# Window attention with its gradients on one core: the order of the first loads and of the weight products

## The chip, the core and the metric

The kernel runs on one core of a Trainium2 chip. The core has five engines that run their own streams of instructions in order: TensorE (PE, matrix products and transposes by product), VectorE (DVE), ScalarE (ACT), GpSimd (POOL) and SyncE (SP). SP, ACT and POOL can issue transfers between the chip's main memory and the core's memory (SBUF), and SP and ACT also transfers that transpose. PE writes to PSUM, which this kernel uses as a ring of eight banks; DVE and ACT copy from there to SBUF. The metric is the time of one execution in microseconds on the device: the median of the runs.

## The reference, cut to what matters

The input x has 256 x 256 positions of 384 channels in bf16, and attention runs in windows of 8 x 8 positions. Wanted are the output, and the gradients of x, wqkv and wo for a given gradient of the output.

```
xw  = x cut into windows of 64 positions           # 1024 windows
q, k, v = split(xw @ wqkv)                          # each 64 x 384
p   = softmax(q @ k.T * 384 ** -0.5)
out = (p @ v) @ wo, put back in place
out, grads of (x, wqkv, wo) by jax.vjp for grad_out
```

## The kernel before, in words

**Products of weights.** The kernel never forms q, k and v. With A = scale * Wq Wk^T the scores are x A x^T, and with B = Wv Wo the output is p (x B); the gradient uses the transposes AT and BT in the same way. So the weights are loaded once (`w_sb` holds wqkv with column blocks 0, 1, 2 for q, k, v; `wo_sb` holds wo), turned block by block (`turn_blocks`, nine PE transposes, three copies), and multiplied (`weight_product`, nine products of 384 columns, three copies): BT_sb from wo_sb and the turned v block, A_sb from the turned q and k blocks. B_sb and AT_sb are BT_sb and A_sb turned once more (`weight_rest`, L113, called by the first `step` at L368).

**Quads.** Eight windows, 512 positions in four pieces of 128, make a quad; there are 128 quads (L410), numbered from 0 here as in the code. For each quad the x piece `xq` and the gradient piece `dq` are loaded, four transfers each, and both are needed turned as well (`xT`, `dT`, channels on partitions). `load_turn` (L142) lets SP issue a transposing transfer for that, unless the quad's number is below G_ON_PE (for dT) or X_ON_PE (for xT), L408. With 2 and 1, PE turns the gradients of quads 0 and 1 and the x of quad 0, in `turn_on_pe` (L150): twelve transposes, copies by DVE and ACT in turn (L87).

**The work on a quad.** `project` with kind 0 makes z from BT_sb and dT, with kind 1 makes y from A_sb and xT: nine products of 512 columns each, copied by ACT into `yz`. `gather` (DVE) packs them into `zy`, and `to_tokens` (L182, SP, a transposing transfer) turns them into `tok`. `scores` multiplies yz and xT, `soft` is the softmax and its gradient on DVE, `uv` multiplies xT with B_sb and AT_sb, and `attend` makes the outputs, which POOL stores. Sums for the weight gradients run in between (`gf_rows`, `gf_halves`) from the fourth step on, and the end makes the weight gradients of them.

**The loop.** `step` (L485 to L490) does the second half of quad i-1 (`attend`), the middle of quad i (scores, softmax, uv) and the projections of quad i+1, and loads quad i+4 ahead (AHEAD = 4), though not in the first step. Before each step SP issues the transposing transfers of quad i+2 and then `to_tokens` of quad i.

**The start.** All engines are under a manual schedule (L454): each runs its instructions in the order in which the program names them. ACT issues v, wo and q (L76 to L78). SP issues quad 0's gradient, the k columns, quad 0's x (L128 to L131), then x of quads 1 and 2 (L140), the turn of quad 1's x (L147), x of quads 3 and 4 (L140), and in the loop the turns of quad 2 and tok of quad 0 (L184). POOL clears the sums, then makes a copy of one column (L132) that holds it until quad 0's first x piece is there, and then issues the gradients of quads 1 to 4 (L138). PE makes seven products of zeros (`warm_up`), then turns v, turns quad 0's gradient, makes BT_sb, turns q, makes z of quad 0, turns k, turns quad 0's x, makes A_sb, turns quad 1's gradient, makes y of quad 0, and enters the loop, where it turns BT_sb and A_sb first.

Of the kernel before, what the change touches and what calls it, by code (L numbers as in the profile page):

```python
# [11 lines left out]
BF16 = mybir.dt.bfloat16  # L12
# [11 lines left out]
def kernel(  # L24
# [47 lines left out]
    def columns(k):  # L72
        return slice(k * C, (k + 1) * C)

    def fetch_weights():
        nc.scalar.dma_start(out=w_sb[:, :, columns(2)], in_=w_in[:, :, columns(2)])  # L76
        nc.scalar.dma_start(out=wo_sb[:], in_=wo.rearrange("(m p) n -> p m n", p=P))
        nc.scalar.dma_start(out=w_sb[:, :, columns(0)], in_=w_in[:, :, columns(0)])  # L78

    def warm_up(n):  # L80
        zero = B_sb[:].rearrange("p m c -> p (m c)")[:, 0:4 * P]
# [11 lines left out]
    def turn_blocks(dst, src, first=0, act=True):  # L93
        for k in range(CK):
            pt = ring.tile([P, C], BF16, tag="r", name="pt")
            for m in range(CK):
                nc.tensor.transpose(pt[:, m * P:(m + 1) * P], src[:, m, (first + k) * P:(first + k + 1) * P], ident[:])  # L97
            copy_out(k if act else 0, dst[:, k, :], pt[:])

    def weight_product(dst, left, right, sc):  # L100
        for mr in range(CK):
            pc = ring.tile([P, C], F32, tag="r", name="pc")
            for mc in range(CK):
                nc.tensor.matmul(pc[:], lhsT=left[:, mc, mr * P:(mr + 1) * P], rhs=right[:, mc, :],  # L104
                                 start=(mc == 0), stop=(mc == CK - 1))
            if sc is not None and mr % 2:
                nc.scalar.activation(out=dst[:, mr, :], in_=pc[:], func=ACT.Copy, scale=sc)
            elif sc is not None:
                nc.vector.tensor_scalar(out=dst[:, mr, :], in0=pc[:], scalar1=sc, scalar2=None, op0=ALU.mult)
            else:  # L110
                copy_out(mr, dst[:, mr, :], pc[:])

    def weight_rest():  # L113
        turn_blocks(B_sb, BT_sb)
        turn_blocks(AT_sb, A_sb)

    def windows(ap, st, first, count=2):
        row, col = st["at"]
        return ap[0, row + WIN * first:row + WIN * (first + count), col:col + WIN, :]
# [4 lines left out]
    def load_first(st):  # L124
        st["xq"] = xq = grp.tile([P, QUAD, C], BF16, tag="xq", name="xq", bufs=2 * GQ + 5)
        st["dq"] = dq = qp.tile([P, QUAD, C], BF16, tag="dq", name="dq", bufs=6)
        for t in range(QUAD):
            nc.sync.dma_start(out=dq[:, t, :], in_=windows(grad_out, st, 2 * t))  # L128
        nc.sync.dma_start(out=w_sb[:, :, columns(1)], in_=w_in[:, :, columns(1)])
        for t in range(QUAD):  # L130
            nc.sync.dma_start(out=xq[:, t, :], in_=windows(x, st, 2 * t))  # L131
        nc.gpsimd.tensor_copy(out=spare[:], in_=xq[:, 0, 0:1])  # L132

    def load(st):
        st["xq"] = xq = grp.tile([P, QUAD, C], BF16, tag="xq", name="xq", bufs=2 * GQ + 5)
        st["dq"] = dq = qp.tile([P, QUAD, C], BF16, tag="dq", name="dq", bufs=6)
        for t in range(QUAD):
            nc.gpsimd.dma_start(out=dq[:, t, :], in_=windows(grad_out, st, 2 * t))  # L138
        for t in range(QUAD):
            (nc.gpsimd if st["i"] == AHEAD + 1 else nc.sync).dma_start(out=xq[:, t, :], in_=windows(x, st, 2 * t))  # L140
# [9 lines left out]
    def turn_on_pe(st, src, dst):  # L150
        for t in range(QUAD):
            pt = ring.tile([P, CK, P], BF16, tag="r", name="pt")
            for m in range(CK):
                nc.tensor.transpose(pt[:, m, :], st[src][:, t, m * P:(m + 1) * P], ident[:])
            copy_out(t, st[dst][:, t, :, :], pt[:])
# [6 lines left out]
    def project(st, kind, mo):  # L162
        if kind == 0 and mo == 0:
            st["yz"] = qp.tile([P, CK, QUAD, 4, WT], BF16, tag="yz", name="yz", bufs=1)
        yz = st["yz"]
        wgt, src = ((BT_sb, st["dT"]), (A_sb, st["xT"]))[kind]
        pj = ring.tile([P, QUAD, 2, WT], F32, tag="r")
        for m in range(CK):
            product(pj[:].rearrange("p t w k -> p (t w k)"), wgt[:, m, mo * P:(mo + 1) * P], src[:, :, m, :],
                    m == 0, m == CK - 1)  # L170
        if kind == 0:
            ENG[EV["z"][mo]](out=yz[:, mo, :, 0:4:3, :], in_=pj[:])  # L172
        else:
            ENG[EV["y"][mo]](out=yz[:, mo, :, 1:3, :], in_=pj[:])  # L174

    def gather(st, kind):
        if kind == 0:
            st["zy"] = qp.tile([P, 2, CK, QUAD, 2, WT], BF16, tag="zy", name="zy")
        src = st["yz"][:, :, :, 0:4:3, :] if kind == 0 else st["yz"][:, :, :, 1:3, :]
        nc.vector.tensor_copy(out=st["zy"][:, kind, :, :, :, :], in_=src)  # L180
# [180 lines left out]
    def step(c, b, a, ahead):  # L361


        def on(st):
            return (lambda f, *r: f(st, *r)) if st is not None else (lambda f, *r: None)
        C_, B, A = on(c), on(b), on(a)
        if b is not None and c is None:
            weight_rest()  # L368
        B(scores)
        B(soft, 0)  # L370
        B(uv, 0, 0)
        B(uv, 0, 1)
        B(soft, 1)
        B(uv, 1, 0)
        B(uv, 1, 1)
        B(soft, 2)
        B(soft, 3)
        B(uv, 2, 0)
        B(uv, 2, 1)
        B(uv, 3, 0)  # L380
        B(uv, 3, 1)
        B(soft, 4)
        for mo in range(CK):
            A(project, 0, mo)
        B(soft, 5)
        if b is not None and not b["on_pe"]:
            turn(b)
        if b is not None and b["i"] == 1:
            turn_blocks(woT_sb, wo_sb, act=False)
        if ahead is not None:  # L390
            load(ahead)
        A(gather, 0)
        for mo in range(CK):
            A(project, 1, mo)
        for rows in range(1 if a is not None else 2):
            if fill:
                gf_rows(*fill.pop(0))
        if b is not None and b["on_pe"]:
            turn(b)
        slots = attention(c) if c is not None else iter(())  # L400
        for t in range(QUAD):
            if t == 2:
                A(gather, 1)
            next(slots, None)
        for rest in slots:
            pass

    G_ON_PE, X_ON_PE = 2, 1  # L408
    EV = {"z": "AAA", "y": "AAA", "u": "AAAA", "v": "AAAA", "o": "AAAA", "U": "DDDD", "W": "AAAA", "d": "DADAA"}
    quads = [(row, col) for col in range(0, W, WIN) for row in range(0, H, 2 * WIN * QUAD)]  # L410
    n = len(quads)
# [41 lines left out]

    with tc.manual_schedule(engines=MANUAL):  # L454
        spare = sm.tile([P, 1], BF16, name="spare", bufs=1)
        fetch_weights()
        warm_up(7)
        nc.scalar.copy(out=spare[:], in_=B_sb[:, 0, 0:1])
        make_identity(nc, ident[:])
        nc.gpsimd.memset(GF_acc[:], 0.0)  # L460
        load_first(sts[0])
        load(sts[1])
        load(sts[2])
        load_turn(sts[0])
        load_turn(sts[1])
        load(sts[3])
        load(sts[4])
        turn_blocks(wT[2], w_sb, 2 * CK)
        turn_on_pe(sts[0], "dq", "dT")
        weight_product(BT_sb, wo_sb, wT[2], None)  # L470
        turn_blocks(wT[0], w_sb, 0)
        for mo in range(CK):
            project(sts[0], 0, mo)
        turn_blocks(wT[1], w_sb, CK)
        turn_on_pe(sts[0], "xq", "xT")
        gather(sts[0], 0)
        weight_product(A_sb, wT[0], wT[1], scale)
        turn_on_pe(sts[1], "dq", "dT")
        for mo in range(CK):
            project(sts[0], 1, mo)  # L480
        gather(sts[0], 1)
        held = []
        last = None
        get = lambda i: sts[i] if 0 <= i < n else None
        for i in range(n + 1):  # L485
            if 0 <= i < n - 2:
                load_turn(sts[i + 2])
            if 0 <= i < n:
                to_tokens(sts[i])
            step(get(i - 1), get(i), get(i + 1), get(i + AHEAD) if i else None)  # L490
            if i > 0:
                held.append(sts[i - 1])
                sts[i - 1] = None
            if held and i == n:
                last = gf_final(held)
            elif len(held) == GQ:
                fill.extend((held, f, ma) for f in range(2) for ma in range(CK))
                held = []
        while fill:
            gf_rows(*fill.pop(0))  # L500
        weight_gradients(last)
# [30 lines left out]
```

## Time and profile before

| what | value |
|---|---|
| runs, median (lowest to highest of 3) | 1904.01 us (1903.54 to 1905.97) |
| the profiled execution | 1900.77 us |
| its span, first to last instruction | 1899.0 us |
| PE busy | 1889.7 us, 100% of the span, 22413 products |
| DVE busy | 1664.4 us, 88% |
| ACT busy | 1526.1 us, 80% |
| POOL busy | 862.7 us, 45% |
| DMA, mean rate | 215 GB/s, 407.69 MB |
| transposing transfers, median to landing | dT 7.9 us, xT 7.5 us, tok 7.7 us |
| plain loads, median to landing | x 4.1 us (SP), gradient 5.9 us (POOL) |
| first transfers: issued, landed | v 0.74, 4.0; wo 1.19, 5.2; q 1.73, 8.1; k 3.39, 9.0 |
| quad 0's gradient, four pieces | issued from 0.74, landed 4.3 to 7.9 |
| quad 0's x, four pieces | issued from 4.02, landed 9.3 to 10.1 |
| scores of quad 0 on PE | start at 19.86 us |
| projections of quad 1 | z at 24.49 us, y at 26.44 us |

How to read it: all times behind the third line are counted from the span's start. A transfer has a moment of issue on its engine and a moment of landing, at which the waiting engine is told. PE's busy time is that of products whose ends are modelled, so that a busy PE need not be at its peak; the chain of waits tells better what sets the end.

### The profile page before, as it was taken

Reading aid. Unit: us, or ns where it says so; the run is one execution under the profiler, and the core shown is the slowest. Engines: PE = TensorE matmul, PEld = TensorE weight load, DVE = VectorE, ACT = ScalarE, POOL = GpSimd, SP = SyncE. Lnnn points to the kernel's source line nnn. Section 1 sums busy time; section 2 is a strip of 40 time slices with the busy share of each in tenths; the row PEclk is TensorE's granted clock in tenths of the full one; section 3 lists DMA queues with packets and bytes.
Section 4 is the critical chain, followed back from the end, with each engine's and each line's share of the span. In section 5 each row is a group of like instructions: output and inputs, shape, how many; then the busy total and the mean of one; then the engine's idle time right before and its main releaser. Section 6 shows DMA issues by size and latency. Waiting matters only on the chain.

```text
span 1899.0 us, 57224 instructions
## 1 busy us (share of the span) xinstructions
PE 1889.7 (100%) x22413; PEld 1127.3 (59%) x22413; DVE 1664.4 (88%) x3606; ACT 1526.1 (80%) x3348; POOL 862.7 (45%) x1576
## 2 busy tenths in 40 slices
PE   9999999999999999999999999999999999999999
PEld 5565566556655665566556555655565566556655
DVE  5888888888888888888888888888888888888887
ACT  7888878887887888788878887888788878888884
POOL 4445445444454454444444544544444444444532
PEclk9999999999999999999999999999999999999999
DMA  9999999999999999999999999999999999999994
GB/s 214 234 224 216 218 219 223 216 211 207 233 221 213 223 218 219 220 211 223 212 222 222 215 219 208 230 206 220 224 219 216 221 218 203 229 219 217 222 185 98
DMA packets 946511, 407.69 MB, mean 215 GB/s; under 512 B 828480, under 2 KB 921664, under 8 KB 946240
## 3 DMA queue, kind: packets, MB, share of 16 engines
q1 hardware_dynamic: 869632, 251.94, 77.6%
q0 software_dynamic: 75264, 151.11, 31.7%
q8 instruction: 175, 2.87, 0.6%
q10 hardware_dynamic: 1344, 0.98, 0.2%
q14 instruction: 96, 0.79, 0.1%
HBM read 101.84 MB, written 101.84 MB: 107 GB/s over the span
## 4 chain that ended last, share of the span: by engine, by line
PE 99%; DVE 1%; DMA 0%; SPq 0%; issue 0%; ACT 0%
PE pj L158 52%; PE pg L158 13%; PE ph L339 13%; PE sd L158 5%; PE pw L284 5%; PE po L284 4%; PE pu L284 4%; PE pd L284 1%; PE pe L421 0%; DMA dq<-in_grad_out_dram 0%; PE pc L104 0%; PE pt L97 0%; DVE Uq L298 0%; DVE Wq L295 0%; DVE d L288 0%; SPq L128 0%
## 5 line engine op out<-in xcount | busy, mean ns | idle before, releaser
L304 POOL DMA_DIRECT2D out_dram<-o x512 | 273.6, 534 | 919.0 <-ACT o L288 904.5
L295 ACT CAST Wq<-pw 128x384 bf16<-128x384 f32 x506 | 243.8, 482 | 275.7 <-PE pw L284 275.3
L158 PEld LDWEIGHTS <-xT 128*128 128x128 bf16 x3072 | 291.8, 98 | 182.2
L158 PE MATMUL pj<-B_sb,xT 128*128 128x384 bf16 x1536 | 333.4, 326 | 0.0
L158 PE MATMUL pj<-AT_sb,xT 128*128 128x384 bf16 x1536 | 333.3, 326 | 0.0
L138 POOL DMA_DIRECT2D dq<-in_grad_out_dram x508 | 268.7, 542 | 73.5 <-PE pj L158 24.8
L298 DVE CAST Uq<-pu 128x384 bf16<-128x384 f32 x512 | 283.0, 553 | 13.7 <-PE pu L284 1.4
L306 POOL DMA_DIRECT2D out_dram<-d x480 | 278.6, 580 | 15.6 <-ACT uq L242 5.1
L158 PE MATMUL pj<-dT,BT_sb 128*128 128x512 bf16 x1152 | 269.5, 379 | 0.0
L158 PE MATMUL pj<-xT,A_sb 128*128 128x512 bf16 x1152 | 269.5, 379 | 0.0
L172 ACT CAST yz<-pj 128x512 bf16<-128x512 f32 x384 | 224.7, 586 | 37.9 <-PE pj L158 29.3
L284 PE MATMUL pd<-tok,ps 64*64 64x384 bf16 x2048 | 254.4, 326 | 0.0
L288 ACT CAST o<-po 128x384 bf16<-128x384 f32 x512 | 249.6, 488 | 1.5 <-PE po L284 1.4
L242 ACT CAST vq<-pj 128x384 bf16<-128x384 f32 x512 | 247.0, 482 | 3.2
L242 ACT CAST uq<-pj 128x384 bf16<-128x384 f32 x512 | 244.3, 477 | 3.5 <-PE pj L158 1.7
L174 ACT CAST yz<-pj 128x512 bf16<-128x512 f32 x384 | 225.1, 586 | 24.1 <-PE pj L158 0.6
L259 DVE STREAM_TRANSPOSE PS<-ps 32x256 bf16<-32x256 bf16 x492 | 214.5, 436 | 9.4
L158 PEld LDWEIGHTS <-xq 128*128 128x128 bf16 x1572 | 153.6, 98 | 115.3 <-issue 0.9
L339 PEld LDWEIGHTS <-xq 64*64 64x64 bf16 x6000 | 175.9, 107 | 67.9
L339 PE MATMUL ph<-Wq,xq 64*64 64x384 bf16 x3984 | 204.2, 322 | 0.0
L158 PEld LDWEIGHTS <-A_sb 128*128 128x128 bf16 x1152 | 112.6, 98 | 135.4
L158 PEld LDWEIGHTS <-BT_sb 128*128 128x128 bf16 x1152 | 112.7, 98 | 122.1 <-DVE BT_sb L91 0.2
(96 smaller groups left out, 3055.9 us busy)
## 6 DMA issues: line engine op xcount, KB each, us to landing
out_dram<-o POOLq DMA_DIRECT2D x512, 96.0 KB, 3.9
xq<-in_x_dram SPq DMA_DIRECT2D x508, 96.0 KB, 4.1
dq<-in_grad_out_dram POOLq DMA_DIRECT2D x508, 96.0 KB, 5.9
out_dram<-d POOLq DMA_DIRECT2D x480, 96.0 KB, 4.2
out_dram<-d POOLq DMA_DIRECT2D x64, 48.0 KB, 4.4
tok<-zy SPq DMA_TRANSPOSE x128, 7.7
xT<-xq SPq DMA_TRANSPOSE x127, 7.5
dT<-dq SPq DMA_TRANSPOSE x126, 7.9
```

The costliest lines, as they stand in the source:

```text
L138: nc.gpsimd.dma_start(out=dq[:, t, :], in_=windows(grad_out, st, 2 * t))
L158: nc.tensor.matmul(out, lhsT=lhsT, rhs=rhs, start=start, stop=stop)
L172: ENG[EV["z"][mo]](out=yz[:, mo, :, 0:4:3, :], in_=pj[:])
L174: ENG[EV["y"][mo]](out=yz[:, mo, :, 1:3, :], in_=pj[:])
L242: cp(out=dst[:, t, :], in_=pj[:])
L284: nc.tensor.matmul(dst[o, :], lhsT=operand(st, lhs, t, h), rhs=operand(st, rhs, t, h), **flags)
L288: copies[EV[name][i]](out=sb[rows, :], in_=src[rows, :])
L295: copies[EV["W"][t] if st["i"] >= GQ else "DA"[t % 2]](out=st["Wq"][:, t, :], in_=pw[:])
L298: copies[EV["U"][t]](out=st["Uq"][:, t, :], in_=pu[:])
L304: nc.gpsimd.dma_start(out=windows(out_0, st, 2 * t), in_=o)
L306: nc.gpsimd.dma_start(out=windows(out_1, st, 2 * t - 1), in_=d if t else above[:])
L339: nc.tensor.matmul(dst[o, :], lhsT=st["xq"][h, t, ma * P + o.start:ma * P + o.stop], rhs=st["UW"[f] + "q"][h, t, :], start=(i == 0), stop= ...
```

## The change

The edits all lie in the start and in one constant. `fetch_weights` loads all weight columns, in six transfers spread over SP and ACT: SP two thirds of v, a third of wo and q; ACT a third of v, two thirds of wo and k. `load_first` issues quad 0's gradient alternately from SP and ACT, behind the weights, and no longer loads k; POOL's copy reads the gradient and no longer x. ACT's first copy, which brings its function table with it, moves behind `load_first` and writes a tile of its own. G_ON_PE is 1 instead of 2, so quad 1's gradient is turned by a transposing transfer on SP and no longer by PE. On PE the order becomes: turn v, make BT_sb, turn q, turn k, make A_sb, turn BT_sb into B_sb, and only then turn quad 0's gradient, make z, turn quad 0's x, make y, and turn A_sb into AT_sb; `weight_rest` goes. The loads of quads 3 and 4 leave the start: quad 3's stands in the loop behind quad 0's `to_tokens`, and quad 4's is the load ahead of the first step.

```diff
     def fetch_weights():
-        nc.scalar.dma_start(out=w_sb[:, :, columns(2)], in_=w_in[:, :, columns(2)])
-        nc.scalar.dma_start(out=wo_sb[:], in_=wo.rearrange("(m p) n -> p m n", p=P))
-        nc.scalar.dma_start(out=w_sb[:, :, columns(0)], in_=w_in[:, :, columns(0)])
+        wo_in = wo.rearrange("(m p) n -> p m n", p=P)
+        nc.sync.dma_start(out=w_sb[:, 0:2, columns(2)], in_=w_in[:, 0:2, columns(2)])
+        nc.scalar.dma_start(out=w_sb[:, 2, columns(2)], in_=w_in[:, 2, columns(2)])
+        nc.scalar.dma_start(out=wo_sb[:, 0:2, :], in_=wo_in[:, 0:2, :])
+        nc.sync.dma_start(out=wo_sb[:, 2, :], in_=wo_in[:, 2, :])
+        nc.sync.dma_start(out=w_sb[:, :, columns(0)], in_=w_in[:, :, columns(0)])
+        nc.scalar.dma_start(out=w_sb[:, :, columns(1)], in_=w_in[:, :, columns(1)])
...
-    def weight_rest():
-        turn_blocks(B_sb, BT_sb)
-        turn_blocks(AT_sb, A_sb)
...
         for t in range(QUAD):
-            nc.sync.dma_start(out=dq[:, t, :], in_=windows(grad_out, st, 2 * t))
-        nc.sync.dma_start(out=w_sb[:, :, columns(1)], in_=w_in[:, :, columns(1)])
+            (nc.sync, nc.scalar)[t % 2].dma_start(out=dq[:, t, :], in_=windows(grad_out, st, 2 * t))
         for t in range(QUAD):
             nc.sync.dma_start(out=xq[:, t, :], in_=windows(x, st, 2 * t))
-        nc.gpsimd.tensor_copy(out=spare[:], in_=xq[:, 0, 0:1])
+        nc.gpsimd.tensor_copy(out=spare[:], in_=dq[:, 0, 0:1])
...
-        if b is not None and c is None:
-            weight_rest()
...
-    G_ON_PE, X_ON_PE = 2, 1
+    G_ON_PE, X_ON_PE = 1, 1
...
         spare = sm.tile([P, 1], BF16, name="spare", bufs=1)
+        warm = sm.tile([P, 1], BF16, name="warm", bufs=1)
         fetch_weights()
         warm_up(7)
-        nc.scalar.copy(out=spare[:], in_=B_sb[:, 0, 0:1])
         make_identity(nc, ident[:])
         nc.gpsimd.memset(GF_acc[:], 0.0)
         load_first(sts[0])
+        nc.scalar.copy(out=warm[:], in_=B_sb[:, 0, 0:1])
         load(sts[1])
         load(sts[2])
         load_turn(sts[0])
         load_turn(sts[1])
-        load(sts[3])
-        load(sts[4])
         turn_blocks(wT[2], w_sb, 2 * CK)
-        turn_on_pe(sts[0], "dq", "dT")
         weight_product(BT_sb, wo_sb, wT[2], None)
         turn_blocks(wT[0], w_sb, 0)
+        turn_blocks(wT[1], w_sb, CK)
+        weight_product(A_sb, wT[0], wT[1], scale)
+        turn_blocks(B_sb, BT_sb)
+        turn_on_pe(sts[0], "dq", "dT")
         for mo in range(CK):
             project(sts[0], 0, mo)
-        turn_blocks(wT[1], w_sb, CK)
         turn_on_pe(sts[0], "xq", "xT")
         gather(sts[0], 0)
-        weight_product(A_sb, wT[0], wT[1], scale)
-        turn_on_pe(sts[1], "dq", "dT")
         for mo in range(CK):
             project(sts[0], 1, mo)
+        turn_blocks(AT_sb, A_sb)
         gather(sts[0], 1)
...
-            step(get(i - 1), get(i), get(i + 1), get(i + AHEAD) if i else None)
+            if i == 0:
+                load(sts[AHEAD - 1])
+            step(get(i - 1), get(i), get(i + 1), get(i + AHEAD))
```

## The prediction, made before the changed kernel was run

> **What bounds the kernel now.** I read the page first, then the chain of waits in time order for the first 30 us, then busy time and granted clock per stretch, then the order of ACT, SP and POOL with each transfer's time to landing.
>
> ```profile
> span 1899.0 us, 57224 instructions
> ...
> PE 99%; DVE 1%; DMA 0%; SPq 0%; issue 0%; ACT 0%
> ```
>
> The page's span, and the share of each engine in the chain that ended last: TensorE (PE) holds 99% of it. Between 100 and 1800 us PE is busy in 1700.00 of 1700.00 us and no PE wait is listed; a quad takes 14.57 us (the row of 42 projections starts at 83.30, 97.86, 112.43). The change touches nothing that runs there, so it can only shift the moment from which this train runs. My measuring point is the start of quad 0's scores: 19.86 us in the order of time. What comes behind follows at fixed distances, unless a transfer is late.
>
> ```profile
> 2.75 5.13 DMA dq<-in_grad_out_dram
> ...
> 7.93 0.50 PE pt L154 x3
> 8.43 2.88 PE pc L104 x9
> 11.31 0.52 PE pt L97 x9
> 11.83 1.94 PE pj L158 x9
> 13.77 0.50 PE pt L97 x9
> 14.28 0.67 PE pt L154 x12
> 14.95 1.46 PE pc L104 x9
> 16.41 0.67 PE pt L154 x12
> 17.08 1.94 PE pj L158 x9
> 19.02 1.00 PE pt L97 x18
> 20.03 0.70 PE sd L158 x24
> ```
>
> This is the chain before that point (start, length, what). PE waits for the fourth piece of quad 0's gradient (lands 7.88), and from then on it never waits. Nine products of L104 take 2.88 us the first time and 1.46 the second: same shape, another clock.
>
> ```profile
> core 0: us, PE busy (x) PEld busy (x) DVE busy (x) ACT busy (x) POOL busy (x), PEclk, DMA share, GB/s
> 0.98:4.39 3.41, 3.19 (x10) 1.23 (x11) 0.16 (x1) 1.48 (x2) 2.25 (x2) 1.00 0.72 208
> 4.39:7.81 3.42, 1.40 (x18) 0.88 (x16) 1.09 (x4) 0.96 (x2) 0.00 (x0) 1.00 1.07 291
> 7.81:11.22 3.41, 3.29 (x14) 1.78 (x15) 0.79 (x2) 0.96 (x2) 1.36 (x3) 0.50 0.75 190
> ```
>
> The granted clock (PEclk) is 0.50 from 7.81 to 11.22 and 1.00 behind it. The stretch ahead of the slow one had PE busy 1.40 of 3.42 us (41%); the ones ahead of full clock 3.19 (93%) and 3.29 (96%). So a stretch of 3.41 us seems to set the clock of the next, with a threshold between 41% and 93%.
>
> **What the change removes.** The wait for the gradient: PE has weight work from 4.2 us on. The 12 transposes of quad 1's gradient on PE (0.67 us, at 16.41). Cover: B_sb and AT_sb are turned (2 x 0.50) in either version, B_sb earlier.
>
> **What it puts in the way**, in order of time. Rows used: transposes 0.50 us for 9 and 0.67 for 12; products 1.46 for 9, so 0.163 each; projections 1.94 for 9; copies on DVE 0.35 (bf16) and 0.56 (from f32); on ACT 0.48 (0.44 when queued) and 0.59 (projection); some 0.2 us from a matmul's start to its copy. With the order of before and its landings these rows give 19.9 for the scores, against 19.86.
>
> 1. *Landing of weights.* The v columns came 3.3 us after issue (4.0); in two pieces I take 4.2, as SP's first 96 KB took 3.6 (4.3). wo_sb came 4.0 us after issue, 5.2. Up to 6.11 the DMAs had moved 1.25 x 365 + 2.11 x 291 = 1070 KB since 2.75 and some 130 KB before it, and all weights are 1180 KB: q and k columns land by about 7, against 8.1 and 9.0. Quad 0's gradient follows them, at about 7.9 as now; x still by 10.1. Both then have slack. PE turns v at 4.2 to 4.75.
> 2. *ACT.* It issues three transfers until 2.24 today, then loads its table (1.28) and copies (0.19), free at 3.75. Now two pieces of gradient stand ahead of the table load. The transfer at L131 held SP for 0.9 us until an early piece of gradient had landed: SP and ACT seem to share eight places for transfers in flight. ACT's second piece is the tenth, so ACT stands until one of the first two has landed, 3.5 to 4.4. Then 0.55 + 1.28 + 0.19: free at 5.5 to 6.4; without such a wait at 5.0 (3.4 + 1.28 + 0.19, rounded up). I take 5.85. Behind it ACT's queue holds the middle third of the turned v, ready at 6.35.
> 3. *First product.* Its second matmul needs that third: 6.4 + 8 x 0.163 = 7.7 (between 6.8 and 8.2). The wait of PE is thus turned from the gradient to ACT, about 1.6 us of it.
> 4. *q and k turned*, 2 x 0.50: 8.7. Now DVE binds: from 7.9 on it has the last third of BT_sb (0.56) and four copies of 0.31 to 0.35, and the next product waits for the third of these, until 9.4. Before, a projection of 1.94 us lay there as cover. Product: 9 x 0.163 = 1.46, until 10.9.
> 5. *B_sb* 0.50, 11.4; gradient turned 0.67, 12.05. Now DVE still has A_sb's last third, two copies of B_sb, two of dT: PE waits 0.9 us, to 12.95, where before the first product was the cover. Projection 1.94: 14.9.
> 6. *x turned* 0.67: 15.55. ACT still has the last projection copy (0.59) and two copies of xT (0.88): PE waits 1.1 us, to 16.65; before, the second product and quad 1's turn covered it. Projection: 18.6. AT_sb turned 0.50: 19.1; the last projection copy ends 19.5.
>
> Sum: the scores start at 19.5 instead of 19.86, so -0.35 us. With ACT free at 5.0 it is 18.7 (-1.2), with 6.4 it is 20.05 (+0.2).
>
> **Queues behind it.** SP has 17 issues ahead of its first transpose in both versions (4 + 1 + 12 before; 3 + 2 + 12 after), so it gets there at about 12.5. It then needs quad 1's gradient from POOL. POOL's copy now waits for a piece of gradient (7.3) instead of x (9.3), so its issues start near 7.9, not 10.04, and the fourth piece lands near 13.7 instead of 15.83. Then dT of quad 1, xT, dT, xT and tok of quad 0, at 2.7 us of issue each: starts 13.7, 16.4, 19.1, 21.8, 24.5. To landing they took 7.7, 8.9, 8.4 and 9.3 us. So dT lands at 22.6 or sooner against its need at 24.1 (19.5 + 4.63, the distance in the trace); xT at 25.0 against 26.1; tok at 33.8 against 38.1 (38.44 before, and tok landed 36.78). The eight x transfers of quads 3 and 4, which took SP from 14.71 to 21.50, now stand behind tok: that is why quad 0's tok gains time, and why what is late next is quad 3's dT (33.64 before, 35 to 37 now) and through it quad 1's tok: 38.33 before, landed 47.33; now 40 to 41.5, landing at 49 to 50.5, needed at 50.8 (51.17 before). It fits, with 0.3 us at the tight end. POOL's later loads only move forward. I cost the queues at nothing; if that slack is gone, each us late costs one.
>
> **The clock.** The stretch 4.39 to 7.81 would hold half of v's turn, the first product and the start of q's, about 1.95 us (57%): between 41% and 93%, so the trace does not decide. The forecast takes full clock. At half clock from 7.81 to 11.22 the sum gives 20.6 (+0.75).
>
> The Trainium skill's page "TensorE: Matmul & The Clock Gate", section "Part 4: PE-mode transpose", says that transposes do not count as PE activity in the way matmuls do. By that rule the first stretch would count 1.46 us at most (43%), which speaks for the half clock and, as later stretches are a third transposes, for a second one. This trace cannot tell: its slow stretch followed one that held transposes and much idling.
>
> **Rivals.**
>
> *One slow stretch*, from 7.81: +0.75 us (+0.2 with ACT at 5.0, +1.2 at 6.4), slower than before, 1904.8. It decides from a busy share in the stretch before that lies under the unknown threshold. For it: the same stretch is slow today. Against: twice as many products in it.
>
> *Two or three slow stretches*: idling in 11.2 to 14.6 (0.9 us) keeps the clock down there too. Scores at 22.0 (two) or 23.5 (three): +2.2 or +3.6, 1906 to 1908. Against it: the stretch ahead is about 70% busy.
>
> *SP late by one transpose*: quad 1's dT adds 2.7 us to a queue whose rest does not get shorter soon. If quad 1's tok lands 1 to 2 us after its need, PE stands there for it: +0.7 to +1.7 us net, 1905. For: the 0.3 us above; against: today's x transfers stood up to 1.5 us for a free place, which the later order need not repeat.
>
> *The wait just goes*: ACT's transfers find free places and copies are quicker than I queue them, scores at 18.2 to 18.7: -1.2 to -1.7, 1902.5. More than that is excluded: even from 6.8 (first product) the remaining PE work is 9.2 us (1.0 + 1.46 + 0.5 + 0.67 + 1.94 + 0.67 + 1.94 + 0.5 + 0.5 for the copy), so not under 16.0, and the copies that queue behind each turn exclude that.
>
> **How the numbers follow.** The profiled execution took 1900.77 (span 1899.0 and 1.77 around it); the median of the runs is 1904.01, 3.24 more, so I carry differences over to the median: 1904.0 - 0.4 = 1903.6. Chances: the forecast 0.45, one slow stretch 0.25, two or three 0.10, SP late 0.12, the wait just goes 0.08. Their times reach from 1902.3 to 1907.6; runs of before lie between 1903.54 and 1905.97, so 1.2 us more on the lower side, and the far tail of the slow stretches left out: 1901.0 to 1907.0. The forecast's own range is 1902.6 to 1904.4. 0.2% (3.8 us) is about what a measurement of this kernel can tell from no change; a gain of that size needs scores at 16.1, below every case but noise: 0.06. A loss of that size needs three slow stretches, or two and a late transpose: 0.10. Within it: 0.84.
>
> **What would show it.** First product after the wait for ACT's copy of the turned v (a table load behind two more issues); PE idle ahead of the second product, and ahead of both projections, ended by DVE or ACT; granted clock 1.00 from 7.8 to 11.2; scores near 19.5; no PE wait for dT, xT or tok of quads 1 and 2; 14.57 us a quad after 80 us. I am wrong if scores start below 18 or above 21, if PE waits for a transpose, or if the train after 100 us has gaps.

## The result and the profile after

The changed kernel is slower: 1909.78 us median of 6 runs (1906.35 to 1911.87), the kernel before beside it 1903.1 us (6 runs); the ratio is 1.0035, 95% interval 1.0022 to 1.0048. The profiled execution took 1911.87 us, the longest of its six; its span is 1910.1 us, 11.1 us above that of before.

The page's span and the chain that ended last, by engine:

```profile
span 1910.1 us, 57200 instructions
...
PE 97%; DMA 2%; DVE 1%; POOL 0%; ACT 0%; issue 0%; SPq 0%; DVEq 0%
```

DMA, at 0% of the chain before, now holds 2% of 1910 us. Where those lie is seen in the start of the scores of each quad on PE (us from the span's start):

| quad | before | after | difference |
|---|---|---|---|
| 0 | 19.86 | 19.61 | -0.25 |
| 1 | 28.84 | 32.79 | +3.95 |
| 2 | 42.39 | 46.34 | +3.95 |
| 3 | 55.13 | 65.42 | +10.29 |
| 4 | 67.86 | 78.66 | +10.80 |
| 127 | 1859.42 | 1870.22 | +10.80 |

The start got 0.25 us shorter, and 11 us are lost, nearly all in two steps, between quads 0 and 1 and between 2 and 3. Behind 80 us nothing changes any more: between 100 and 1800 us PE is again busy in 1700.00 of 1700.00 us.

PE in order of time ahead of quad 0's scores (start, length, what, and in brackets PE's wait before the first of a group and who ended it):

```profile
5.86 1.46 PE L108 MATMUL pc<-wT,wo_sb 128*128 128x384 bf16 x8 [0.41 <-ACT wT L93]
8.81 1.18 PE L101 MATMUL pt<-ident,w_sb 128*128 128x128 bf16 x18 [1.48 <-DMA w_sb<-in_wqkv_dram]
10.20 1.64 PE L108 MATMUL pc<-wT 128*128 128x384 bf16 x9 [0.22 <-DVE wT L95]
...
13.63 2.10 PE L157 MATMUL pj<-dT,BT_sb 128*128 128x512 bf16 x9 [0.61 <-ACT dT L93]
...
17.17 2.10 PE L157 MATMUL pj<-xT,A_sb 128*128 128x512 bf16 x9 [0.77 <-ACT xT L93]
```

The wait for the gradient is gone, and in its place stand waits for ACT's copy of the turned v, for the q columns (landed 8.76), and for the copies ahead of the second product and of each projection. Next, PE's waits between 20 and 60 us by line and by what ended them (us in total, times, longest); before, no transfer stands in this list; the lines for transfers are:

```profile
PE pj L157 <- DMA xT<-xq: 4.4, 2, 2.2
PE pj L157 <- DMA dT<-dq: 1.4, 1, 1.4
```

One of the two for xT is quad 1's, the other quad 3's. Behind 60 us PE waits 2.0 us more for tok. The order on SP tells why (start of issue, its length; first, of the kernel before, quad 3's dT and xT; then, of the changed kernel, quad 1's dT and xT, quad 2's dT and xT, quad 0's tok, x of quads 3 and 4, quad 3's dT and xT, quad 1's tok):

```profile
33.64 3.03 SPq L147 DMA_TRANSPOSE dT<-dq  x1
36.72 1.51 SPq L147 DMA_TRANSPOSE xT<-xq  x1
```

```profile
14.64 2.71 SPq L146 DMA_TRANSPOSE dT<-dq  x1
17.47 6.09 SPq L146 DMA_TRANSPOSE xT<-xq  x1
23.79 4.38 SPq L146 DMA_TRANSPOSE dT<-dq  x1
28.34 3.58 SPq L146 DMA_TRANSPOSE xT<-xq  x1
31.97 6.85 SPq L183 DMA_TRANSPOSE tok<-zy  x1
38.86 5.08 SPq L139 DMA_DIRECT2D xq<-in_x_dram  x8
44.17 1.78 SPq L146 DMA_TRANSPOSE dT<-dq  x1
46.12 3.30 SPq L146 DMA_TRANSPOSE xT<-xq  x1
49.46 6.55 SPq L183 DMA_TRANSPOSE tok<-zy  x1
```

The two rows of before are issued when the last of POOL's loads has landed (33.0), and they land 5.1 and 4.2 us from the start of issue. In the changed kernel quad 1's dT lands 11.4 us after the start of its issue (26.06), its xT 12.9 us (30.3), and the chain of waits names that one, and then quad 1's tok, issued at 49.46 and landed at 61.08:

```profile
17.47 12.86 DMA xT<-xq
...
49.46 11.62 DMA tok<-zy
```

Last, busy time and granted clock (PEclk, third from the end) in the stretches around that wait:

```profile
core 0: us, PE busy (x) PEld busy (x) DVE busy (x) ACT busy (x) POOL busy (x), PEclk, DMA share, GB/s
52.92:56.33 3.41, 1.21 (x6) 0.51 (x6) 0.42 (x1) 0.91 (x3) 0.00 (x0) 1.00 1.13 282
56.33:59.74 3.41, 2.81 (x22) 1.00 (x20) 0.00 (x0) 2.11 (x4) 0.00 (x0) 0.50 1.24 135
```

While PE waits for quad 3's xT it is busy 1.21 of 3.41 us, and the clock is 0.50 from 56.33 to 66.57. The mean clock of the six runs is 0.997 to 0.999.

### The profile page after: what moved, and what is told of

Its sections match the earlier page's. It is cut to its first block, busy times and chain, and to the rows that moved or that the text cites. A ratio compares the mean times of both kernels' runs of the same rounds, so it can differ in the third digit from the quotient of the medians.

```text
span 1910.1 us, 57200 instructions
## 1 busy us (share of the span) xinstructions
PE 1891.9 (99%) x22401; PEld 1127.4 (59%) x22401; DVE 1664.0 (87%) x3604; ACT 1524.1 (80%) x3346; POOL 862.5 (45%) x1576
## 4 chain that ended last, share of the span: by engine, by line
PE 97%; DMA 2%; DVE 1%; POOL 0%; ACT 0%; issue 0%; SPq 0%; DVEq 0%
PE pj L157 51%; PE pg L157 13%; PE ph L338 13%; PE sd L157 5%; PE pw L283 5%; PE po L283 4%; PE pu L283 4%; DMA xT<-xq 1%; DMA tok<-zy 1%; PE pd L283 1%; DMA dq<-in_grad_out_dram 1%; PE pe L418 0%; POOL dq L137 0%; DVE Uq L297 0%; DVE Wq L294 0%; DVE d L287 0%
## 5 line engine op out<-in xcount | busy, mean ns | idle before, releaser
L297 DVE CAST Uq<-pu 128x384 bf16<-128x384 f32 x512 | 283.0, 553 | 13.7 <-PE pu L283 1.3
```

Source lines behind the costliest of these rows:

```text
L297: copies[EV["U"][t]](out=st["Uq"][:, t, :], in_=pu[:])
```

## The experiments

The theory after the first look: quad 1's added transposing transfer sets PE waiting. The rivals: it is the place of the x loads on SP; transposing transfers are slow one behind the other whatever runs beside them; or POOL's loads in flight make them slow. All diffs are against the changed kernel unless said otherwise. "Before" in a set is the kernel before on the same chip: 1901.7 us median in the first and in the second set, 1901.39 in the third.

**Quad 1's gradient back on PE.**

```diff
-    G_ON_PE, X_ON_PE = 1, 1
+    G_ON_PE, X_ON_PE = 2, 1
...
         gather(sts[0], 0)
+        turn_on_pe(sts[1], "dq", "dT")
         for mo in range(CK):
             project(sts[0], 1, mo)
```

> The changed kernel with one part undone: quad 1's gradient is turned by PE again (12 transposes, ahead of the second projection, where PE waited 0.77 us for ACT anyway). Theory (the added transposing transfer is the cause): scores of quad 0 start at 19.6 to 19.9, the first transposing transfer on SP is xT of quad 1 and lands before 24.5, PE waits for no transfer behind 20 us, the clock stays full there, quad 3's scores start within 0.5 us of 55.1 (55.13 before, 65.42 after), so 0.2 to 0.6 us faster than before. Rival (the order of x behind tok is the cause): PE still waits for quad 1's tok near 50 us and half or more of the 10.8 us stays.

Measured: 1903.39 us median of 10 (1900.22 to 1908.82), ratio 1.0008 (0.9996 to 1.0020). In the trace, which is of one of the quickest of these runs (1900.28), scores of quads 0 and 3 start at 18.76 and 54.28 and PE waits for no transfer behind 20 us; the first xT landed at 23.2. The place that the theory names is right and most of the loss is gone, but not the gain of 0.2 to 0.6 us that was expected: the median is 1.7 us above before, with an interval that reaches zero. Quad 0's scores came sooner than the 19.6 to 19.9 expected. Runs of up to 1908.8 us say that something late may be left in a part of them, which this trace doesn't show.

**The added transfer alone, on the kernel before.**

```diff
-    G_ON_PE, X_ON_PE = 2, 1
+    G_ON_PE, X_ON_PE = 1, 1
...
-        turn_on_pe(sts[1], "dq", "dT")
```

> The kernel before with this one part of the change: quad 1's gradient is turned by a transposing transfer instead of by PE. Theory (the added transfer): PE waits for dT or xT of quad 1 by 2 to 5 us, scores of quad 1 start at 30.5 to 33.5 instead of 28.84, and a later wait for a tok follows; in all 4 to 12 us slower than before. Rival (it needs the new order of loads too): PE waits under 1 us, the time stays within 1 us of before.

Measured: 1903.94 us median of 10, ratio 1.0015 (1.0005 to 1.0024): 2.2 us slower than its before, less than the 4 to 12 expected and more than the rival's 1. The trace is again of the quickest run (1901.28): scores of quad 0 at 19.07, of quad 1 at 29.03, one wait of 0.8 us for xT. So neither the expected wait of 2 to 5 us nor a wait for tok is seen; where the median's 2.2 us lie, no trace shows.

**The x of quads 3 and 4 at the start again.**

```diff
         load_turn(sts[1])
+        load(sts[3])
+        load(sts[4])
...
-            if i == 0:
-                load(sts[AHEAD - 1])
-            step(get(i - 1), get(i), get(i + 1), get(i + AHEAD))
+            step(get(i - 1), get(i), get(i + 1), get(i + AHEAD) if i else None)
```

> The changed kernel with the loads of quads 3 and 4 back at the start, where the kernel before has them, ahead of quad 2's turns on SP. Theory (the added transfer, in competition with the loads): PE's waits for dT and xT of quad 1 stay (1 to 3 us each), quad 0's tok lands 3 to 6 us later than its 40.8 and PE waits for it, quad 1's tok comes sooner than 61.1; in all as slow as the changed kernel or slower (1908 to 1914). Rival (x behind tok is what makes quad 1's tok late): the waits behind 45 us go and 5 us or more of the loss with them, 1904 to 1906.

Measured: 1904.75 us median of 10 (1901.89 to 1910.74), ratio 1.0019 (1.0008 to 1.0029). The theory's 1908 to 1914 is wrong, and the rival's 1904 to 1906 holds: the place of the x loads seems to matter too. In the trace (1901.89, the quickest run, where that of the changed kernel is its longest) SP issues quad 2's dT at 27.81 instead of 23.79 and yet quad 3's dT at 37.06 instead of 44.17; quad 1's tok lands at 50.5. Of the waits for transposing transfers, 0.7 us for quad 1's xT is left.

**POOL held until quad 1's xT has landed.** Quad 2's gradient is split from its x, which SP loads as before.

```diff
-        load(sts[2])
+        load(sts[2], g=False)
         load_turn(sts[0])
         load_turn(sts[1])
+        nc.gpsimd.tensor_copy(out=spare[:], in_=sts[1]["xT"][:, 0, 0, 0:1])
+        load(sts[2], x_=False)
```

> The changed kernel with POOL held, behind the gradient of quad 1, until quad 1's xT has landed; the gradients of quads 2 to 5 are issued behind that. Theory A (transposing transfers crawl because POOL's loads are in flight beside them): dT of quad 1 lands within 8 us of its issue instead of 11.4, SP's issue of xT takes under 4 us instead of 6.1, xT lands before 26 instead of 30.3, scores of quad 1 start at 28.5 to 30 instead of 32.8; what comes later can be late for other reasons. Theory B (transposing transfers in a row are slow by themselves): dT and xT land as late as in the changed kernel, within 1.5 us.

Measured: 1914.22 us median of 4, ratio 1.0071 (1.0056 to 1.0086), and theory A in the place that it is about. SP in this run (start of issue, its length; quad 1's dT and xT, quad 2's, quad 0's tok):

```profile
14.56 1.95 SPq L149 DMA_TRANSPOSE dT<-dq  x1
16.64 1.61 SPq L149 DMA_TRANSPOSE xT<-xq  x1
25.09 1.44 SPq L149 DMA_TRANSPOSE dT<-dq  x1
26.70 2.53 SPq L149 DMA_TRANSPOSE xT<-xq  x1
29.28 9.50 SPq L186 DMA_TRANSPOSE tok<-zy  x1
```

Quad 1's dT and xT, one right behind the other with POOL silent, land 4.4 and 3.9 us from the start of issue, against 11.4 and 12.9. Quad 1's scores start at 28.31. So they aren't slow in a row by themselves. Whether the same loads would slow them as much if SP or ACT issued them, no run tests. The held loads then fall on quad 0's tok, whose issue alone takes 9.50 us and which lands 14.4 us from its start, at 43.7; PE waits 10.5 us in two places for tok. The same loads do harm where they are put, which speaks for theory A from the other side.

**The changed kernel once more.**

> The changed kernel as it is, as the control of this set on its chip. Expected 1906 to 1912, with waits of PE for dT and xT of quad 1 and for quad 1's tok, and in most executions a stage at half clock near 56 us (mean clock 0.997 or 0.998).

Measured: 1906.81 us median of 5, ratio 1.0027 (1.0010 to 1.0043). Run by run, time and mean clock: 1903.7 and 1904.15 at 1.000, 1906.81 at 0.999, 1909.81 at 0.998, 1911.43 at 0.997. The trace is of the run of 1904.15: waits of 1.6 us for xT, 0.9 for tok, 0.3 for dT, no stage at half clock. So the waits that were expected are there, but shorter, and a mean clock of 0.997 or 0.998 shows in two of five runs, not in most. The same waits occur in different sizes in one kernel.

**Products of no use in the waits.**

```diff
+    def keep_busy(k):
+        pt = ring.tile([P, 3 * P], F32, tag="r", name="busy")
+        for i in range(k):
+            nc.tensor.matmul(pt[:], lhsT=ident[:], rhs=BT_sb[:, 0, :], start=True, stop=True)
...
         A(gather, 0)
+        if a is not None and a["i"] == 3:
+            keep_busy(12)
         for mo in range(CK):
             A(project, 1, mo)
+        if a is not None and a["i"] == 3:
+            keep_busy(10)
```

> The changed kernel with 12 products of no use ahead of quad 3's second projection and 10 behind it (1.96 and 1.63 us of PE at full clock), where PE stands for quad 3's xT and quad 1's tok. Theory (the waits also cost the clock): the clock stays full from 5 us on, the waits for transfers stay, and the scores of quad 4 lag those of before by 8 to 9 us instead of 10.8 where the waits are as long as in the changed kernel's trace (sum of waits behind 20 us 8 to 9 us). Rival (the half clock lies wholly inside waits and costs nothing): the lag stays at 10.5 us or more with waits as long.

Inconclusive: 1908.54 us median of 4 (1907.51 to 1911.39), ratio 1.0039 (1.0026 to 1.0053), above the control's median and within its range. In the trace the clock is full from 4.9 us on and quad 4's scores lag by 74.31 - 67.86 = 6.45 us, but that execution had 2.2 us of waits, all for quad 1, and the products took most of the rest. The condition of both theories (waits as long as in the changed kernel's trace) didn't come about. From the trace of the changed kernel an estimate: from quad 1's first pd, which waits for tok, to quad 3's scores it is 65.42 - 61.13 = 4.29 us against 55.13 - 51.17 = 3.96 before, and a step further 13.24 against 12.73. By this estimate some 0.8 us of the 10.8 are half clock; the rest came before that pd, which started when tok landed.

**The new order alone.** Both later parts undone: the diffs of the first and the third experiment together.

> The changed kernel with both later parts undone: quad 1's gradient is turned by PE, and the loads of quads 3 and 4 stand at the start. Left are the weights first and PE's new order. Theory (that order is worth what it moves the scores by, and nothing behind is late): scores of quad 0 at 18.7 to 19.6, no wait of PE for a transfer behind 20 us, 0 to 1 us faster than before, and less spread than with x behind tok. Rival (the earlier gradients on POOL make transposing transfers late in any case): waits for xT or tok appear and the time is 1 us or more above before.

Measured: 1901.24 us median of 10 (1900.48 to 1902.17), ratio 0.9995 (0.9986 to 1.0004): no measurable difference, with the least spread of all. Scores of quad 0 at 19.57. PE's waits from 15 to 100 us name no transfer:

```profile
PE po L283 <- DVE Wq L294: 1.2, 3, 0.4
PE pw L283 <- DVE Uq L297: 0.7, 3, 0.2
```

**Turns as cover.** The order alone, and

```diff
-        turn_blocks(B_sb, BT_sb)
         turn_on_pe(sts[0], "dq", "dT")
+        turn_blocks(B_sb, BT_sb)
```

> The same as the run with the order only, with BT_sb's turn moved behind the turn of quad 0's gradient, where it covers the wait for the copies ahead of the first projection (0.6 us). Theory: scores of quad 0 at 18.2 to 19.0, the wait for ACT's dT copy gone, 0.3 to 0.6 us faster than the run with the order only and 0.5 to 1.5 us faster than before. Rival (DVE's and ACT's copies just queue up behind the turn): no gain beyond 0.2 us over the run with the order only.

Measured: 1900.47 us median of 11, ratio 0.9999 (0.9990 to 1.0008). Scores of quad 0 at 18.55; the wait for ACT's dT copy is gone, as expected. The medians are 0.8 us under the order alone and 1.2 under before; the interval doesn't tell it from before.

**x of quads 3 and 4 from POOL.**

```diff
-            (nc.gpsimd if st["i"] == AHEAD + 1 else nc.sync).dma_start(out=xq[:, t, :], in_=windows(x, st, 2 * t))
+            (nc.gpsimd if AHEAD - 1 <= st["i"] <= AHEAD + 1 else nc.sync).dma_start(out=xq[:, t, :], in_=windows(x, st, 2 * t))
```

> The changed kernel with the x of quads 3 and 4 issued by POOL, behind their gradients, instead of by SP behind quad 0's tok (SP loses eight issues, 5.1 us, ahead of quad 3's dT). Theory A (SP's own order: those eight issues delay quad 3's dT and through it quad 1's tok): quad 3's dT is issued right behind quad 0's tok, quad 1's tok lands 5 us or more sooner relative to quad 0's tok than in the control (there 17.6 us apart), no wait of PE for it, 1902.5 to 1905. Theory B (what counts is how many of POOL's loads are in flight beside the transposing transfers): SP's issues of quad 2's turns and of tok grow by what the eight issues gave back, quad 1's tok is as late as in the control or PE waits elsewhere for a transfer, 1906 or more.

Measured: 1911.23 us median of 4 (1909.71 to 1913.17), ratio 1.0052 (1.0038 to 1.0065). SP in this run (quad 2's xT, quad 0's tok, quad 3's dT and xT, quad 1's tok):

```profile
26.64 4.78 SPq L146 DMA_TRANSPOSE xT<-xq  x1
31.47 8.70 SPq L183 DMA_TRANSPOSE tok<-zy  x1
40.41 4.57 SPq L146 DMA_TRANSPOSE dT<-dq  x1
45.15 2.47 SPq L146 DMA_TRANSPOSE xT<-xq  x1
47.67 4.09 SPq L183 DMA_TRANSPOSE tok<-zy  x1
```

Quad 1's tok lands 9.8 us behind quad 0's instead of 17.6 in the control, as A has it, and PE doesn't wait for it. But quad 0's tok lands at 46.9 instead of 36.5, and PE waits 4.7 us for that, besides 2.4 us for quad 1's xT and 0.6 for its dT: B decides. By the medians, 9.8 us above before against 5.1 in the control, eight loads taken from SP and put in flight from POOL cost more than their place on SP; the two intervals just overlap.

**ACT's table load first.** The turns as cover, and

```diff
-        load_first(sts[0])
         nc.scalar.copy(out=warm[:], in_=B_sb[:, 0, 0:1])
+        load_first(sts[0])
```

> The run with turns as cover, with ACT's first copy (and so its table load) ahead of its two pieces of gradient. Theory: ACT is free near 3.75 instead of 5.3, the wait for ACT's copy of the turned v goes, and as the q columns then bound the next turn (landing 8 to 8.8 before) the scores of quad 0 start 0 to 0.5 us sooner than in that run; the median within 1 us of its 1900.47, and 0.5 to 2 us under before. Rival: the later gradient pieces make quad 0's gradient late and PE waits for it, scores not sooner.

Measured: 1900.27 us median of 11, ratio 0.9996 (0.9987 to 1.0005); scores of quad 0 at 18.73, against 18.55: not sooner. The wait ahead of the first product did not go: ACT's two pieces of gradient, now behind the table load, hold it from 4.00 to 5.50. PE still waits 0.4 us for ACT's copies, and 0.4 instead of 0.8 us for the q columns. The median is 1.1 us under before, again within the interval.

**The parts together** (median less that of before in its set, us):

| | x loads at the start | x loads behind tok |
|---|---|---|
| quad 1's gradient turned by PE | -0.5 | +1.7 |
| turned by a transposing transfer | +3.0 | +5.1 |

By these medians the transfer costs 3.4 to 3.5 us and the place of the x loads 2.1 to 2.2. From the intervals of the ratios the four cells reach from -2.7 to 0.8 and from -0.8 to 3.8 in the first row, from 1.5 to 5.5 and from 1.9 to 8.2 in the second. So the transfer's cost is clear of noise with x at the start, and the experiment on the kernel before, with 2.2 us, agrees; the place of the x loads is not shown by times alone. The first six runs of the changed kernel gave +6.7 for the last cell, so that the two simply add up is not shown either. The new order of weights and products, which is most of the diff, costs nothing and brings nothing that can be measured.

## Why the prediction was wrong

It said 1903.6 us, no measurable change, within 1901.0 to 1907.0. Point by point:

- **The sum up to the scores held, in part by luck.** 19.61 measured, 19.5 worked out. ACT was free at 5.43 (5.5 to 6.4 expected): its second piece of gradient, the ninth transfer of SP and ACT and not the tenth, was issued at 3.38, just behind the landing of the first (3.35), and SP's second, the tenth, at 3.85, behind the landing of the second (3.83). So the eight shared places behave as read, and each seems to be reused in the order of issue. The waits for copies were 0.61 and 0.77 us ahead of the projections (0.9 and 1.1 expected), 0.22 ahead of the second product (0.7) and 0.41 ahead of the first (1.6). One term was missed: the q columns landed at 8.76, not by 7, among the pieces of gradient issued behind them (8.4 to 9.4), and PE waited 1.48 us. The sum stands because these errors cancel.
- **The clock held where it was in question.** It stayed full from 5.13 to 56.33; the rivals of one to three slow stretches in the start didn't occur. The rule of the Trainium skill's page "TensorE: Matmul & The Clock Gate", section "Part 4: PE-mode transpose", that transposes don't count as PE activity in the way matmuls do was given as speaking for a slow stretch; none came behind 5.13 to 8.54, where PE was busy 52% of the time, mostly with products, and none behind 8.54 to 11.95, where nearly half of PE's work was transposes. That does not refute the rule: the products alone fill 1.64 of those 3.41 us, 48%, more than the 41% that was followed by half clock.
- **"I cost the queues at nothing" failed.** The forecast let no transfer be late, and quad 3's dT went out at 44.17 instead of 35 to 37, quad 1's tok landed at 61.08 instead of 49 to 50.5. The step that broke is the one ahead of that cost: transposing transfers "at 2.7 us of issue each: starts 13.7, 16.4, 19.1, 21.8, 24.5", landing 7.7 to 9.3 us later. Measured starts: 14.64, 17.47, 23.79, 28.34, 31.97; to landing 11.4 and 12.9 us for the first two. Durations were taken from rows of before as if they belonged to the instruction, but they depend on what is in flight beside it: 4.4 and 3.9 us with POOL silent. The trace of before already held both prices, 7.7 to 8.9 us for the dT and xT issued among POOL's loads and 5.1 and 4.2 for quad 3's, issued behind them. The same paragraph let POOL start its gradients 2.1 us earlier and called it "only forward". In truth they started 0.9 us earlier (9.13 instead of 10.04), and they are what the transfers crawl beside. The earlier start alone does no harm that shows: in the run of the new order alone POOL starts at 9.27, and no wait for a transfer follows.
- **The rival "SP late by one transpose" is what happened**, with 0.12 of the chance and too low a price. It named a right victim, quad 1's tok, and gave 0.7 to 1.7 us; medians lose 5.1 to 6.7. Two things were left out of its price. First, quad 1's dT and xT were given 1.1 to 1.5 us of slack (1.3 to 1.5 by the rows themselves, as 16.4 + 8.4 is 24.8 and not 25.0), and PE waited 1.4 and 2.2 us for them. Second, the eight x loads were counted as costing their issue time anywhere. At the start they took SP 6.59 us (experiment with x up front), but they held quad 2's dT and xT and quad 0's tok back to 27.81, behind the last of POOL's loads (issued at 24.4), and those three then took SP 8.9 us; in the changed kernel they took 14.8 us, and 11.2 in its second trace, with 5.08 and 5.71 us of x loads still to come in front of quad 3's dT. The medians put that at 2.1 us, which is within their noise.
- **A threshold between 41% and 93% for the clock** was right to leave open, but the prediction looked for its effect in the start alone. It struck where a wait for a transfer had opened a gap, at 56 us.

What stays open: how much of each longer execution the half clock adds (the products of no use didn't settle it); why waits of the changed kernel differ so much between executions (7.8 us for transfers behind 20 us in one trace, 2.8 in the other); and why four of ten executions with the gradient on PE and x behind tok lie 3 to 7 us above the median of before, since the only trace of that kernel is of a quick one. Why loads from POOL slow a transposing transfer is open too.

## What to carry to other kernels

Don't give a transposing transfer one duration: in the first 60 us of these traces dT and xT took 3.8 to 12.9 us. Price it with what will be in flight beside it in the new order, and ask of every load that moves which transposing transfers it will meet. A turn that PE can do in 0.67 us inside a wait that is there anyway was cheaper here than one more transfer on a queue that is nearly full. When loads are moved behind a queue's transposing transfers to make room, ask what these will then run beside: here they moved forward into POOL's loads, and most of the room was used up by longer issues.

## What the runs showed of the hardware that was not expected

- Two transposing transfers in a row take 4.4 and 3.9 us to landing with no load from POOL in flight, 11.4 and 12.9 us with thirteen of POOL's 96 KB loads issued between 14.6 and 30.3 us. In the kernel before, with the order alone and with x up front, quad 3's dT and xT, issued with no such load in flight, took 3.8 to 5.1 us. It was 14.4 us for the larger tok (29.28 to 43.7) in the run with POOL held and then let go. SP's issue grows with it: 1.6 to 2.0 us, 2.7 to 6.1, 9.5.
- It is not a matter of bytes alone: in the changed kernel the DMAs moved 97 GB/s from 18 to 24 us with a busy share of 1.07, in the kernel before 253 GB/s at the same share.
- The clock fell to half behind stretches of 3.41 us with PE busy 41% (before, 4.39 to 7.81) and 35% (after, 52.92 to 56.33), and stayed full behind 45% (1.55 us, x from POOL, 25.92 to 29.33) and 52% (after, 5.13 to 8.54). It stayed at half behind one that was busy 82% (2.81 us, after, 56.33 to 59.74) and came back behind one that was busy 83% (x from POOL, 46.40 to 49.81). PE's busy share as the profile models it therefore does not decide alone at half clock.
